# A local-attention block with a gated feed-forward: the feed-forward's units in pairs, two first products and then two second ones, with the transposes between them

## The chip, the cores and the metric

The kernel runs on one core of one Trainium2 chip. The metric is the device time of one execution in microseconds (us); the figures given are medians of several runs. A profiled execution is one run of its own: its span counts from the first to the last instruction of the program, its time also has what lies around them.

## The reference

`x` has 2048 tokens of 640 features. It is normalised, and the result `xn` goes two ways: through a local attention (32 heads of 20 features, a window of 8 keys at every second position) with the output projection `wo`, and through a feed-forward with 1536 hidden features. The two are multiplied and added to `x`:

```python
xn = _layernorm(x)
s  = attention(xn @ wqkv) @ wo        # keys at pos - 2*w, w = 0..7
g  = silu( silu(xn @ w1) @ w2 )       # w1: 640 x 1536, w2: 1536 x 640
return x + s * g
```

All tensors are float32.

## The kernel before, in words

**Precision.** Each float32 operand is split into a high part rounded to the matmul type float32r and a low part (the rest). A product is three matmuls: high by high, low by high, high by low. Tiles come in such pairs: `TH`/`TL` (transposed normalised tokens, or transposed attention output), `SH`/`SL` (hidden features after silu), and a weight slot of the ring `WR` (seven slots, each with both halves of one weight unit).

**Groups.** The 2048 tokens are worked in four groups of 512 (four tiles of 128 rows). For each group TensorE does a qkv phase, from the second group on the `wo` phase of the group before, and then the feed-forward phase `ffn_phase`. After the last group comes the last `wo` product, `wo_last`. VectorE does the attention itself (long multiplies and reductions, L477 to L517) while TensorE is in the later phases.

**The feed-forward phase.** The hidden features go in 12 units of 128. For unit f there is a *first product* (below U): 15 matmuls of 512 columns into one PSUM bank of `ROT` (L786 to L788), with a slice of w1 as the stationary operand and `TH`/`TL` as the moving one. ScalarE then takes silu of the bank twice, into `SH[f % 2]` (rounded) and `SF[f % 2]` (exact), and VectorE subtracts the two into `SL[f % 2]` (L792 to L794). And there is a *second product* (below D): for each of the four token tiles, the stationary operand is 128 tokens of `SH` or `SL`, the moving one the 640 columns of w2's unit, in a matmul of 384 columns (L667) and one of 256 (L669), both in `tm_mm`. D has 16 matmuls with `SH` (`big`: by w2's high, then by its low half) and 8 with `SL` (`small`). All twelve D of a group accumulate in the same six PSUM banks of `ACC`, which ScalarE empties through silu into `G` at the end (L823).

**The order before.** U runs one unit ahead of D: U0, U1, D0, U2, D1, and so on to U11, D10, D11. In D the eight `small` matmuls come last, but for D11, where each token tile has its big and small ones together.

**Transposes.** Five chunks per group are transposed by four TensorE transposes each into a bank of `ROT` (L429 in `split_t`; below T), and leave it by a ScalarE copy into `TH` (L433) and a VectorE subtraction into `TL` (L434). In the first three groups they are the next group's normalised tokens, ahead of U7 to U11 (`XT_AT`). In the last group they are chunks of the attention output `O`, ahead of U8 to U11 and, for the fifth, ahead of D11 (`OL_AT`). `ROT` has two banks, taken in turn by U and T.

**Who sets the order.** Every operation is put on record with the tiles that it reads and writes. `Weave` plans starting times with a table of costs and then emits the instructions; TensorE keeps the order in which its work was recorded, the others are ordered by the plan and by priorities. Weight units are loaded in the order of the list `units`, seven ahead (`w_load`, called by `w_done` when a unit has been used); the first group loads raw weights, splits them on ScalarE and VectorE or GpSimd and stores them, later groups load the stored halves by GpSimd's queue (L363).

Of the kernel before, what the change touches and what calls it, by code (L numbers as in the profile page):

```python
# [8 lines left out]
F32 = mybir.dt.float32  # L9
F32R = mybir.dt.float32r  # L10
AF = mybir.ActivationFunctionType
OP = mybir.AluOpType
# [38 lines left out]
def tsl(t):  # L51
    return slice(t * P, (t + 1) * P)
# [120 lines left out]
def local_attention_silu_ffn(ctx: ExitStack, tc: tile.TileContext, x, wqkv, wo, w1, w2, out):  # L173
# [62 lines left out]
    def rot():  # L236
        i = take("rot", 2)
        return ROT[i], ("rot", i)
# [7 lines left out]
    def dve(n, fn, reads, writes, prio, lock=False):  # L246
        add("DVE", dv(n), fn, reads, writes, prio, lock)

    def act(n, fn, reads, writes, prio, table=None):
        add("ACT", ac(n), fn, reads, writes, prio, table=table)  # L250

    def pe(dur, fn, reads, writes):
        add("PE", dur, fn, reads, writes)
        clock[0] += dur
# [22 lines left out]
    for g in range(NG):  # L277
        units += [("q", q, c) for q in range(NQ) for c in range(DC)]
        if g:
            units += [("wo", c) for c in range(DC)]  # L280
        for f in range(FC + 1):
            if f < FC:
                units.append(("w1", f))
            if f:
                units.append(("w2", f - 1))
    units += [("wo", c) for c in range(DC)]
    again = {u: sum(v == u for v in units) for u in units}
    halves = {}
# [97 lines left out]
    def w_next(*want):  # L386

        i = used[0]
        assert units[i] == want and i < loaded[0], (units[i], want)
        used[0] += 1  # L390
        s, n, at = i % RING, width(want), start(want)
        return WR[s][:, at:at + n], WR[s][:, D + at:D + at + n], ("wh", s), ("wl", s)

    def w_done(n=1):
        for _ in range(n):
            w_load()


    def load_x(g, t, n=1, prio=None):
        dma(lambda: nc.sync.dma_start(XIN[:, t:t + n], rows(xg, g)[:, t:t + n]), [],  # L400
            [("xin", u) for u in range(t, t + n)], n * P * D * 4, clock[0] if prio is None else prio)

    def ln_stats(t, after=()):
        st = ST[t % 2]
        ks = ("st", t % 2)
        for k in range(2):
            dve(320, lambda k=k: nc.vector.bn_stats(out=st[:, k, :], in_=XIN[:, t, k * 320:(k + 1) * 320]),
                [("xin", t), *after], [ks + (k,)], 1)
        dve(60, lambda: nc.vector.bn_aggr(out=MV[:, t, :], in_=st), [ks + (0,), ks + (1,)], [("mv", t)], 1)

    def ln_rstd(a, b, at=1):
        n = range(a, b)
        act(b - a, lambda: nc.scalar.activation(SD[:, 0, a:b], MV[:, a:b, 1], AF.Sqrt, bias=epst, scale=1.0),
            [("mv", t) for t in n], [("sd", t) for t in n], 0, "sqrt")
        dve(10, lambda: nc.vector.reciprocal(out=SD[:, 1, a:b], in_=SD[:, 0, a:b]),
            [("sd", t) for t in n], [("rs", t) for t in n], at)

    def ln_apply(t):
        dve(320, lambda: nc.vector.tensor_scalar(
            out=XIN[:, t, :], in0=XIN[:, t, :], scalar1=MV[:, t, 0:1], scalar2=SD[:, 1, t:t + 1],  # L420
            op0=OP.subtract, op1=OP.mult), [("rs", t), ("mv", t)], [("xin", t)], 1, lock=True)

    def split_t(src, skeys, c, i):

        ps, kp = rot()

        def turn():
            for t in range(T):
                nc.tensor.transpose(ps[:, tsl(t)], src[:, t, c * P:(c + 1) * P], ident)  # L429
        pe(0.54, turn, skeys, [kp])  # L430
        hi, lo = TH[i][:, c, :], TL[i][:, c, :]
        kh, kl = t_keys(i, [c], kinds=["th"]), t_keys(i, [c], kinds=["tl"])
        act(TOK, lambda: nc.scalar.activation(hi, ps, AF.Copy), [kp], kh, 0)  # L433
        dve(TOK, lambda: nc.vector.tensor_tensor(out=lo, in0=ps, in1=hi.bitcast(F32), op=OP.subtract),  # L434
            [kp] + kh, kl, 0)
# [85 lines left out]
    def o_chunk(g, c, i):  # L521
        qs = range(c * P // CQ, ((c + 1) * P - 1) // CQ + 1)
        split_t(O, [("o", q, t) for q in qs for t in (0, 2)], c, i)
# [127 lines left out]
    def t_keys(i, cs, ts=range(T), kinds=("th", "tl")):  # L651
        return [(k, i, c, t) for k in kinds for c in cs for t in ts]

    O_AT = {(1, 1): 0, (1, 4): 1, (2, 3): 2, (3, 1): 3, (3, 3): 4}
    OL_AT = {8: 0, 9: 1, 10: 2, 11: 3, 12: 4}
    XT_AT = 7

    def tm_banks():
        a = [bank() for t in range(T)]
        b = [bank() for t in range(T // 2)]  # L660
        return a, b
# [10 lines left out]
    def tm_views(banks):  # L672

        a, b = banks
        for k in range(T // 2):
            for t in (2 * k, 2 * k + 1):
                yield a[t][0][:, :CA].rearrange("p (t m) -> p t m", t=1), a[t][1], slice(t, t + 1), slice(0, CA)
            yield b[k][0].rearrange("p (t m) -> p t m", t=2), b[k][1], slice(2 * k, 2 * k + 2), slice(CA, D)
# [80 lines left out]
        leave(t, B)  # L759

    def ffn_phase(g, i, ix, io):
        nxt = g + 1 if g + 1 < NG else None
        ps = prev = None
        for f in range(FC + 1):
            if nxt is not None and f == 0:
                load_x(nxt, 0, 2)
                load_x(nxt, 2, 2)
                for t in range(T):
                    ln_stats(t)
                ln_rstd(0, T)  # L770
                for t in range(T):
                    ln_apply(t)
            if nxt is not None and XT_AT <= f < XT_AT + DC:
                split_t(XIN, [("xin", t) for t in range(T)], f - XT_AT, ix)
            if nxt is None and f in OL_AT:
                o_chunk(g, OL_AT[f], io)
            cur = None
            if f < FC:
                wh, wl, kh, kl = w_next("w1", f)
                h, kp = rot()  # L780
                s = f % 2

                def first(wh=wh, wl=wl, h=h):
                    for c in range(DC):
                        cs = tsl(c)
                        nc.tensor.matmul(h, wh[:, cs], TH[i][:, c, :], start=c == 0, stop=False)  # L786
                        nc.tensor.matmul(h, wh[:, cs], TL[i][:, c, :], start=False, stop=False)  # L787
                        nc.tensor.matmul(h, wl[:, cs], TH[i][:, c, :], start=False, stop=c == DC - 1)  # L788
                pe(15 * mm(TOK), first, t_keys(i, range(DC)) + [kh, kl], [kp])
                w_done()  # L790
                sf, sh, sl = SF[s], SH[s], SL[s]
                act(TOK, lambda sh=sh, h=h: nc.scalar.activation(sh, h, AF.Silu), [kp], [("sh", s)], 0, "silu")  # L792
                act(TOK, lambda sf=sf, h=h: nc.scalar.activation(sf, h, AF.Silu), [kp], [("sf", s)], 0, "silu")
                dve(TOK, lambda sf=sf, sh=sh, sl=sl: nc.vector.tensor_tensor(  # L794
                    out=sl, in0=sf, in1=sh.bitcast(F32), op=OP.subtract), [("sf", s), ("sh", s)], [("sl", s)], 0, lock=True)
                cur = sh, sl, ("sh", s), ("sl", s)
            if f:
                sh, sl, ksh, ksl = prev
                if ps is None:
                    ps = tm_banks()  # L800
                a, b = ps
                wh, wl, kh, kl = w_next("w2", f - 1)
                for t in range(T):
                    def big(t=t, f=f, wh=wh, wl=wl, sh=sh):
                        tm_mm(ps, t, sh[:, tsl(t)], wh, f == 1, False)
                        tm_mm(ps, t, sh[:, tsl(t)], wl, False, False)

                    def small(t=t, f=f, wh=wh, sl=sl):
                        tm_mm(ps, t, sl[:, tsl(t)], wh, False, f == FC)
                    ko = [a[t][1], b[t // 2][1]]  # L810
                    pe(2 * TM, big, [ksh, kh, kl], ko)
                    if f == FC:
                        pe(TM, small, [ksl, kh], ko)
                    else:
                        late.append((TM, small, [ksl, kh], ko))
                for args in late:
                    pe(*args)
                late.clear()
                w_done()
            prev = cur  # L820
        for p, kp, ts, cs in tm_views(ps):
            n = (ts.stop - ts.start) * (cs.stop - cs.start)
            act(n, lambda p=p, ts=ts, cs=cs: nc.scalar.activation(G[:, ts, cs], p, AF.Silu), [kp], gkeys(ts, cs), 0, "silu")  # L823

    late = []
    add("POOL", 0.7, consts, [], ["consts"], 0)
    act(1, lambda: nc.scalar.activation(SD[:, 1, 0:1], epst, AF.Sqrt), ["consts"], [("rs", 0)], 0, "sqrt")
    slot = 0
# [38 lines left out]
```

## Time and profile before

| | |
|---|---|
| median of 3 runs | 642.76 us (641.28 to 643.1) |
| profiled execution, time | 641.45 us |
| its span | 639.6 us |
| granted TensorE clock, mean over the span | 0.999 |
| busy: TensorE, weight loads, VectorE, ScalarE, GpSimd | 632.7, 572.5, 538.7, 207.2, 123.4 us |
| matmuls, transposes among them | 3495 |

The profiled execution has 1.85 us around its span. Records of matmuls overlap, since they are pipelined: the distance from one start to the next is the pace, the length of a record is not. In a line of the timeline the first number is the start, the second the length of the record, both in us; a line can stand for several instructions of a kind (x4).

### The profile page before, as it was taken

The numbers are of one execution on the slowest core, as the hardware profiler recorded it, in microseconds if no ns is written. First come the engines' busy times: TensorE is split into PE (matmuls) and PEld (weight loads), VectorE is DVE, ScalarE is ACT, GpSimd is POOL, SyncE is SP. The second block draws the span as 40 slices with busy tenths as digits, with TensorE's granted clock in tenths as the row PEclk, the third lists the DMA queues.
The fourth block names the chain that finished last, engine by engine and source line by source line (L and its number), as shares of the span: only waits on it lengthen the run. The fifth ranks groups of instructions, "written<-read, shape, count | busy, mean of one in ns | idle before, by whom it ended". The sixth has DMA issues, their size and how long they took to land.

```text
span 639.6 us, 9015 instructions
## 1 busy us (share of the span) xinstructions
PE 632.7 (99%) x3495; PEld 572.5 (90%) x3495; DVE 538.7 (84%) x539; ACT 207.2 (32%) x401; POOL 123.4 (19%) x168
## 2 busy tenths in 40 slices
PE   7999999999999999999999999999999999999997
PEld 6888889999889989999888999999988899899997
DVE  6699999999999989999839998999106999899814
ACT  4436453443534022324332112223313222233230
POOL 4500000001101241111222125111222213411100
PEclk9999999999999999999999999999999999999999
DMA  9999999777999998657699978865679995885522
GB/s 280 338 306 318 335 403 378 293 233 225 282 328 323 291 303 256 194 167 214 183 267 276 291 219 272 304 186 165 170 208 258 285 301 194 270 305 185 186 83 82
DMA packets 74154, 162.44 MB, mean 254 GB/s; under 512 B 5648, under 2 KB 47088, under 8 KB 74112
## 3 DMA queue, kind: packets, MB, share of 16 engines
q0 software_dynamic: 26672, 82.58, 44.9%
q1 hardware_dynamic: 47040, 79.05, 39.7%
q8 instruction: 27, 0.44, 0.3%
q10 hardware_dynamic: 400, 0.25, 0.1%
q14 instruction: 15, 0.12, 0.1%
HBM read 109.55 MB, written 34.16 MB: 225 GB/s over the span
## 4 chain that ended last, share of the span: by engine, by line
PE 98%; DVE 1%; DMA 1%; ACT 0%; issue 0%; SPq 0%
PE acc L667 22%; PE acc L669 15%; PE acc L633 10%; PE acc L634 10%; PE acc L635 10%; PE rot L788 9%; PE rot L786 9%; PE rot L787 9%; PE rot L429 2%; PE acc L579 2%; DMA xin<-in_A_x_dram 1%; PE rot L756 0%; DVE xin L549 0%; PE rot L558 0%; DVE st L544 0%; ACT th L562 0%
## 5 line engine op out<-in xcount | busy, mean ns | idle before, releaser
L633 PE MATMUL acc<-w,th 128*128 128x480 f32 x300 | 114.7, 382 | 0.0
L667 PE MATMUL acc<-w,sh 128*128 128x384 f32 x384 | 113.6, 335 | 0.0
L634 PE MATMUL acc<-w,tl 128*128 128x480 f32 x300 | 113.5, 378 | 0.0
L635 PE MATMUL acc<-w,th 128*128 128x480 f32 x300 | 113.4, 378 | 0.0
L669 PE MATMUL acc<-w,sh 128*128 128x256 f32 x384 | 107.1, 279 | 0.0
L477 DVE TENSOR_TENSOR pr<-q,kv 128x2560 f32<-128x2560 f32 x32 | 90.3, 2821 | 11.6 <-DMA kv<-kv 11.2
L786 PE MATMUL rot<-th,w 128*128 128x512 f32 x240 | 95.4, 398 | 0.0
L788 PE MATMUL rot<-th,w 128*128 128x512 f32 x240 | 94.0, 391 | 0.0
L787 PE MATMUL rot<-tl,w 128*128 128x512 f32 x240 | 93.9, 391 | 0.0
L509 DVE TENSOR_TENSOR pr<-e,kv 128x2560 f32<-128x2560 f32 x32 | 90.3, 2821 | 0.8
L480 DVE TENSOR_REDUCE l<-pr 128x128 f32<-128x2560 f32 x32 | 90.0, 2814 | 0.2
L363 POOL DMA_DIRECT2D w<-half_q x52 | 37.4, 719 | 233.3 <-DVE pr L514 93.5
L514 DVE TENSOR_TENSOR pr<-pr 128x1280 f32<-128x1280 f32 x64 | 76.6, 1197 | 1.1
L792 ACT ACTIVATE sh<-rot 128x512 fp32r<-128x512 f32 x48 | 28.8, 600 | 149.3 <-PE rot L788 146.6
L669 PEld LDWEIGHTS acc<-w,sh 128*128 128x128 f32 x384 | 72.3, 188 | 1.6
L667 PEld LDWEIGHTS acc<-w,sh 128*128 128x128 f32 x384 | 72.1, 188 | 1.7
L363 POOL DMA_DIRECT2D w<-half_w x72 | 38.6, 537 | 179.3 <-PE acc L669 96.4
L635 PEld LDWEIGHTS acc<-w,th 128*128 128x128 f32 x300 | 56.3, 188 | 8.5
L634 PEld LDWEIGHTS acc<-w,tl 128*128 128x128 f32 x300 | 56.4, 188 | 8.0
L633 PEld LDWEIGHTS acc<-w,th 128*128 128x128 f32 x300 | 56.3, 188 | 8.0
L667 PE MATMUL acc<-w,sl 128*128 128x384 f32 x192 | 57.8, 333 | 0.0
L434 DVE TENSOR_TENSOR tl<-rot,th 128x512 fp32r<-128x512 f32 x35 | 23.8, 681 | 38.3 <-ACT th L433 38.2
(88 smaller groups left out, 1002.9 us busy)
## 6 DMA issues: line engine op xcount, KB each, us to landing
w<-half_w POOLq DMA_DIRECT2D x72, 640.0 KB, 5.5
w<-half_q POOLq DMA_DIRECT2D x52, 480.0 KB, 5.1
half_w<-w SPq DMA_DIRECT2D x24, 640.0 KB
half_q<-w SPq DMA_DIRECT2D x20, 480.0 KB
w<-half_wo POOLq DMA_DIRECT2D x15, 640.0 KB, 5.4
kv<-kv SPq DMA_DIRECT2D x16, 560.0 KB
kv<-kv SPq DMA_DIRECT2D x16, 420.0 KB
gate<-in_B_w_dram SPq DMA_DIRECT2D x16, 320.0 KB
```

Source lines behind the costliest of these rows:

```text
L477: dve(2560, lambda t=t: nc.vector.tensor_tensor(out=PR, in0=win(qq[:, t:t + 2, :], W, 0), in1=win(kv[:, 0, t:t + 2, :], W, CQ), op=OP.mult ...
L480: dve(2560, lambda t=t: nc.vector.tensor_reduce(out=l[:, t:t + 2].rearrange("p t w h -> p (t w h)"), in_=PR.rearrange("p t w (h d) -> p (t ...
L509: dve(2560, lambda t=t, v=v: nc.vector.tensor_tensor(out=PR.rearrange("p t w (h d) -> p t (w h) d", d=DH), in0=e[:, t:t + 2].rearrange("p ...
L514: dve(2 * n * CQ, lambda n=n: nc.vector.tensor_tensor(out=PR[:, :, 0:n, :], in0=PR[:, :, 0:n, :], in1=PR[:, :, n:2 * n, :], op=OP.add), [] ...
L633: nc.tensor.matmul(o, hi, wh, start=c == 0, stop=False)
L634: nc.tensor.matmul(o, lo, wh, start=False, stop=False)
L635: nc.tensor.matmul(o, hi, wl, start=False, stop=c == DC - 1)
L667: nc.tensor.matmul(a[t][0][:, :CA], st, w[:, :CA], start=first, stop=last)
L669: nc.tensor.matmul(b[t // 2][0][:, h * CB:(h + 1) * CB], st, w[:, CA:], start=first and h == 0, stop=last, skip_group_check=True)
L786: nc.tensor.matmul(h, wh[:, cs], TH[i][:, c, :], start=c == 0, stop=False)
L787: nc.tensor.matmul(h, wh[:, cs], TL[i][:, c, :], start=False, stop=False)
L788: nc.tensor.matmul(h, wl[:, cs], TH[i][:, c, :], start=False, stop=c == DC - 1)
```

## The change

`ffn_phase` is written anew. The twelve units go in six pairs: U(f), U(f+1), D(f), D(f+1) for even f. A transpose that belongs to f stands between U(f+1) and D(f), one that belongs to f+1 between D(f) and D(f+1); `XT_AT` is now 6 to 10 and `OL_AT` 7 to 11, so that T stands ahead of D6 to D10 in the first three groups and ahead of D7 to D11 in the last. In the last pair of the first three groups the `small` matmuls of D10 are put off until after the `big` ones of D11. In the last group D11 has big and small matmuls of neighbouring token tiles in turn. The list `units`, and with it the order of the weight loads, follows the pairs. The matmuls, transposes and the work of the other engines are the same in number and shape.

```diff
-        for f in range(FC + 1):
-            if f < FC:
-                units.append(("w1", f))
-            if f:
-                units.append(("w2", f - 1))
+        for f in range(0, FC, 2):
+            units += [("w1", f), ("w1", f + 1), ("w2", f), ("w2", f + 1)]
...
-    OL_AT = {8: 0, 9: 1, 10: 2, 11: 3, 12: 4}
-    XT_AT = 7
+    OL_AT = 7, 8, 9, 10, 11
+    XT_AT = 6, 7, 8, 9, 10
...
+        def turns(at):
+            if nxt is not None and at in XT_AT:
+                split_t(XIN, [("xin", t) for t in range(T)], XT_AT.index(at), ix)
+            if nxt is None and at in OL_AT:
+                o_chunk(g, OL_AT.index(at), io)
...
+            if nxt is None and f == FC - 1:
+                order = [(big, 0)] + [v for t in range(1, T) for v in ((big, t), (small, t - 1))]
+            else:
+                order = [(big, t) for t in range(T)]
...
+        for f in range(0, FC, 2):
+            up(f)
+            up(f + 1)
+            turns(f)
+            rest = down(f)
+            if f < FC - 2 or nxt is None:
+                rest()
+            turns(f + 1)
+            last = down(f + 1)
+            if f == FC - 2 and nxt is not None:
+                rest()
+            last()
```

`up(f)` records U and the two silus and the subtraction; `down(f)` records D's big matmuls and returns `rest`, which records its small ones and marks the weight unit as used.

More of the change, by code (lines that the diff above doesn't have):

```diff
@@ L762, in ffn_phase @@
         nxt = g + 1 if g + 1 < NG else None
[L763 to L767, printed above, removed]
-                for t in range(T):
[L769 to L789, printed above, removed]
-                w_done()
[L791 to L820, printed above, removed]
@@ L821, in ffn_phase @@
-        for p, kp, ts, cs in tm_views(ps):
+        if nxt is not None:
+            load_x(nxt, 0, 2)
+            load_x(nxt, 2, 2)
+            for t in range(T):
+                ln_stats(t)
+            ln_rstd(0, T)
+            for t in range(T):
+                ln_apply(t)
+        def turns(at):
[3 more added lines that the diff above has]
+                o_chunk(g, OL_AT.index(at), io)
@@ new lines, in up, with first @@
+        def up(f):
+            wh, wl, kh, kl = w_next("w1", f)
+            h, kp = rot()
+            s = f % 2
+            def first():
+                for c in range(DC):
+                    cs = tsl(c)
+                    nc.tensor.matmul(h, wh[:, cs], TH[i][:, c, :], start=c == 0, stop=False)
+                    nc.tensor.matmul(h, wh[:, cs], TL[i][:, c, :], start=False, stop=False)
+                    nc.tensor.matmul(h, wl[:, cs], TH[i][:, c, :], start=False, stop=c == DC - 1)
+            pe(15 * mm(TOK), first, t_keys(i, range(DC)) + [kh, kl], [kp])
+            w_done()
+            sf, sh, sl = SF[s], SH[s], SL[s]
+            act(TOK, lambda: nc.scalar.activation(sh, h, AF.Silu), [kp], [("sh", s)], 0, "silu")
+            act(TOK, lambda: nc.scalar.activation(sf, h, AF.Silu), [kp], [("sf", s)], 0, "silu")
+            dve(TOK, lambda: nc.vector.tensor_tensor(out=sl, in0=sf, in1=sh.bitcast(F32), op=OP.subtract),
+                [("sf", s), ("sh", s)], [("sl", s)], 0, lock=True)
@@ new lines, in ffn_phase, with down, big, small @@
+        ps = []
+        def down(f):
+            if not ps:
+                ps.append(tm_banks())
+            a, b = ps[0]
+            s = f % 2
+            wh, wl, kh, kl = w_next("w2", f)
+            def big(t):
+                tm_mm(ps[0], t, SH[s][:, tsl(t)], wh, f == 0, False)
+                tm_mm(ps[0], t, SH[s][:, tsl(t)], wl, False, False)
+            def small(t):
+                tm_mm(ps[0], t, SL[s][:, tsl(t)], wh, False, f == FC - 1)
+            out = [[a[t][1], b[t // 2][1]] for t in range(T)]
+            def give(what, t):
+                if what == big:
+                    pe(2 * TM, lambda: big(t), [("sh", s), kh, kl], out[t])
+                else:
+                    pe(TM, lambda: small(t), [("sl", s), kh], out[t])
+            if nxt is None and f == FC - 1:
+                order = [(big, 0)] + [v for t in range(1, T) for v in ((big, t), (small, t - 1))]
+            else:
+                order = [(big, t) for t in range(T)]
+            for v in order:
+                give(*v)
+            def rest():
+                for t in range(T):
+                    if (small, t) not in order:
+                        give(small, t)
+                w_done()
+            return rest
@@ L822, in ffn_phase @@
+        for f in range(0, FC, 2):
[10 more added lines that the diff above has]
+            last()
+        done = ps[0]
+        for p, kp, ts, cs in tm_views(done):
             n = (ts.stop - ts.start) * (cs.stop - cs.start)
             act(n, lambda p=p, ts=ts, cs=cs: nc.scalar.activation(G[:, ts, cs], p, AF.Silu), [kp], gkeys(ts, cs), 0, "silu")
-    late = []
```

## The prediction

> **What bounds the kernel now.** I read the page's busy shares first, then the chain that ended last, then the waits of TensorE (PE).
>
> ```profile
> span 639.6 us, 9015 instructions
> PE 632.7 (99%) x3495; PEld 572.5 (90%) x3495; DVE 538.7 (84%) x539; ACT 207.2 (32%) x401; POOL 123.4 (19%) x168
> PE 98%; DVE 1%; DMA 1%; ACT 0%; issue 0%; SPq 0%
> ```
>
> ```profile
> PE rot L558 <- DVE xin L549: 1.5, 2, 0.8
> PE rot L532 <- POOL ident masks.py:199: 1.4, 1, 1.4
> PE acc L579 <- DVE tl L566: 0.3, 1, 0.3
> ```
>
> The chain is PE for 98% of the span, and every wait of PE (3.2 us in all) is at L532, L558 and L579, in the start of the first group. In the four feed-forward phases PE waits for nobody. So there is no stall for the new order to remove. Its time can only move by the pace of the matmuls (distance from start to start) or by new waits. The granted clock is 0.999, so the clock isn't the lever either.
>
> Does the pace depend on the order? I went through the timeline of PE, in the trace's starts to the ns (the view prints 10 ns). It does, and the pattern repeats from unit to unit within 2 ns:
>
> - U after a D: 3446 ns (15 matmuls; the first nine start 224 to 236 ns apart, the rest 226 to 227).
> - U after a U: only U1 after U0 shows it. The two together take 6824 ns, and the 15 matmuls of U1 keep 226.6 throughout: 3399.
> - D after a U: 2307 for the big part and 1147 for the small, 3454. The first three pairs of a 384 and a 256 take about 293 each, the others 286.6.
> - D after a D: D11 in the first three groups, twelve pairs at 286.6: 3440.
> - T ahead of U: 355 for the transposes and then 3518 for U, 3873 in all.
> - T ahead of D: once in the whole trace, ahead of D11 of the last group, and it looks different:
>
> ```profile
> 613.87 0.33 PE L667 MATMUL acc<-w,sl 128*128 128x384 f32 x1
> 614.04 0.28 PE L669 MATMUL acc<-w,sl 128*128 128x256 f32 x1
> 614.15 0.60 PE L429 MATMUL rot<-ident,o 128*128 128x128 f32 x4
> 614.51 0.42 PE L667 MATMUL acc<-w,sh 128*128 128x384 f32 x1
> 614.77 0.28 PE L669 MATMUL acc<-w,sh 128*128 128x256 f32 x1
> 614.89 0.34 PE L667 MATMUL acc<-w,sh 128*128 128x384 f32 x1
> ...
> 617.59 0.34 PE L667 MATMUL acc<-w,sh 128*128 128x384 f32 x1
> 617.77 0.28 PE L669 MATMUL acc<-w,sh 128*128 128x256 f32 x1
> 617.89 0.34 PE L667 MATMUL acc<-w,sl 128*128 128x384 f32 x1
> 618.07 0.28 PE L669 MATMUL acc<-w,sl 128*128 128x256 f32 x1
> 618.19 0.34 PE L667 MATMUL acc<-w,th 128*128 128x384 f32 x1
> ```
>
> From T's first start (614.15) to the first matmul of the last `wo` product (618.19) pass 4.04 us, to the ns 4036. After the transposes the first pair takes 382 ns, and from 614.89 to 618.19 eleven pairs take 300 each, against 286.6 for such pairs elsewhere. The pace does not recover within the unit. The order inside this D11 isn't the cause: the D11 of the other groups have the same one, come right after D10, and run at 286.6. I read it as a lasting pace: a D that starts right after transposes stays 13.4 ns per pair slow, some 160 ns per unit.
>
> **The sum, part by part.** The model reproduces the phase before. Groups 0 to 2: 6824 + 5 x 3446 (U2 to U6) + 5 x 3873 (T and U7 to U11) + 11 x 3454 (D0 to D10) + 3440 = 84.85 us, and the next group's first matmul does start 84.85 after this phase's (219.80 to 304.65). Last group: 6824 + 6 x 3446 + 4 x 3873 + 11 x 3454 + 4036 = 85.02, as seen (533.17 to 618.19).
>
> *Pairs.* Groups 0 to 2 have U0 and U1 as before, 6824, and five pairs at 3446 + 3399 = 6845. The three D pairs without a T take 3454 + 3440 = 6894 each. That saves 47 ns for each of five U that now follow a U, and 14 for each D that now follows a D.
>
> *Transposes.* T goes from ahead of U to ahead of D6 to D10, at 4036 each, by the one row there is. D11 then follows D10 without transposes between; I let it keep the slow pace, 12 x 300 = 3600. The trace has T ahead of D after a D (here D7 and D9) and not after a U (D6, D8, D10). Bounds for the latter: 4036, and 3890 (355 + 382 + 11 x 286.6) if that pace is left at once. I take 4036, since T's own starts (108 or 109 apart, the last 28 or 29) are the same after a U-sized matmul, a qkv one or a D.
>
> Groups 0 to 2: 6824 + 5 x 6845 + 3 x 6894 + 5 x 4036 + 3600 = 85.51, so +0.66 each. Last group: 6824 + 5 x 6845 + 4 x 3454 (D0, D2, D4, D6) + 3 x 3440 + 5 x 4036 (D7 to D11) = 85.36, +0.34. In all 3 x 0.66 + 0.34 = +2.3 us: the pairs alone save, the five places of T cost more. The U after a slow D could enter cheaper (U0 and U1 after the `wo` phase take 6824, 21 less than 6845): 8 x 0.02 = 0.17 us, left in the range.
>
> *Waits that the order could add*, all taken at nothing, with their cover. Counted from the end of U's last record, before the change `SH` is ready after 0.64 to 2.41 us over all 48 units and `SL` after 1.85 to 5.29. D's big part used to start 6.7 us after it; now it starts after 3.24 (U 3.40 less the 0.16 by which the record outlasts the next start), and the small part 2.31 later, after 5.54. Margins: 0.8 us for `SH`, 0.25 for the worst `SL`. In the last pair of groups 0 to 2 D10's small part is put off, so D11 needs `SH` after 0.36 + 8 pairs (2.49) - 0.16 = 2.69, against 2.41 at worst. `ROT`: T ahead of D6 takes the bank of U6, whose silus end 1.1 to 2.9 us after U6, during U7. U8 takes it two D later. At the end of a group D10's and D11's small parts finish together 1.2 us before qkv, where D11's tiles used to finish one by one. ScalarE empties a 384 bank in 0.49 and a 512 one in 0.60. By these qkv's tiles, 0.65 us apart, find their four banks free since about 0.3, 0.5, 0.1 and 0.4 us. In the last group D11's turns leave `wo_last` its first two banks about when it asks; a wait here is 0.2 at most. Weights: a slot is used seven units after its load was asked for, some 20 us, and a load lands 5.5 us after its issue. The new `units` order and the later `w_done` of D10 (2.3 us) shift GpSimd's loads and SP's raw loads by at most one unit, 3.5 us. If a cover is gone, the price is the wait itself, since PE runs in order and all else of the phase is queued behind it.
>
> A rule speaks against any effect of the pairs. The Trainium skill, in "TensorE: Matmul & The Clock Gate", section "Wait — 56ns, not 53.3ns?", gives the start-to-start time of warm matmuls as their columns at 2.4 GHz plus a fixed 2.5 ns or so, whatever stands around them. By it the order is free and the sum is 0. The trace disagrees: the same 512-column matmul takes up to 236 or 226.6 ns by what came before.
>
> **Against which time.** The profiled execution took 641.45 us, 639.6 of it span; by its own time the changed kernel takes 643.8. It lies 1.3 under the median of 642.76, at the low end of the three runs, so I put the change on the median: 642.76 + 2.3 = 645.1 us. A measurement of this kernel tells about 0.3%, 1.9 us, from no change.
>
> **The rivals.**
>
> *The slow pace does not come, or not after a U* (0.22). For it: D0 to D10 leave their first slow pairs after three; one row is thin. Without it D6 to D10 cost 3890 and D11 3440. I keep the last group's D11 at 4036, as measured. Then groups 0 to 2 change by -0.235 us each and the last by 0.34 - 4 x 0.146 = -0.24: -0.95 in all, 641.8. If it comes only ahead of D7, D9 and the last D11: +0.2, 643.0. Both are within 0.3%.
>
> *The pace knows no order* (0.05): each matmul keeps one distance whatever comes before, nothing moves, 642.8. The rows above (236 and 226.6 for one shape) speak against it. This is what the rule of the Trainium skill's "TensorE: Matmul & The Clock Gate" would make of the change.
>
> *VectorE becomes late* (0.12). Its queue is in order, and it is 84% busy, much of it with multiplies that cannot be interrupted. The page's group of one of them (32 of 2.82 us), and all 48 subtractions into `SL` (shortest, median and longest in ns):
>
> ```profile
> L477 DVE TENSOR_TENSOR pr<-q,kv 128x2560 f32<-128x2560 f32 x32 | 90.3, 2821 | 11.6 <-DMA kv<-kv 11.2
> ```
>
> ```profile
> L794 DVE TENSOR_TENSOR sl<-sf,sh x48: 676/686/1969, 68.7 to 612.1; 128x512 fp32r<-128x512 f32 x48
> ```
>
> With 0.25 us left at worst, one more 2.82 us multiply ahead of a subtraction costs up to 2.6 us. It decides once `SL` is later than 5.54 us. At half of 2.6 once per group it adds 5.2, some 650. Against it: only 3 of the 48 units are later than 4.8 us before.
>
> *Faster* (0.08): T is cheaper ahead of D than the one row says. If the first pair after T came at its usual pace (287 for 382) and no slow pace followed, 19 new places of T ahead of D would save 0.095 each more than in the first rival: -0.95 - 1.8 = -2.75, 640.0. It decides from an extra under about 45 ns. For it: a D's first weights are ready long before. Against it: 382 at 614.51, and U after T has a first distance of 316 too.
>
> **How the numbers follow.** The forecast has the rest, 0.53. Its 2.3 us are just over the bound (2.1 with the cheaper U), so I count 0.46 of it as slower and 0.07 as the same. Slower: 0.46 + 0.12 = 0.58. Same: 0.07 + 0.22 + 0.05 = 0.34. Faster: 0.08. The range runs from 641.4 (the first rival, less 0.4 for the spread of the runs) to 648.0 (the forecast with one wait of 2.6 us, and the spread); it leaves out the faster case and most of the late VectorE. The likeliest case alone is 644.2 to 646.0.
>
> **What would show it.** In the changed trace: U's second of a pair at 3.40 us; twelve pairs at 300 ns in D6 to D11, 85.5 us from a phase's first matmul to the next phase's, and no wait of PE outside the first group. I am wrong if D after T runs at 286.6, if PE waits for `sl`, `sh` or `gate`, or if a phase is shorter than 84.85.

## The result and the profile after

| | before | after |
|---|---|---|
| median of 5 runs, us | 642.75 (641.28 to 643.1) | 646.28 (645.68 to 647.09) |
| ratio, 95% interval | | 1.0063 (1.0053 to 1.0074) |
| profiled execution, us | 641.45 | 645.68 |
| its span, us | 639.6 | 643.9 |

The change makes the kernel slower by 3.5 us in the medians. The forecast was 645.1, 2.3 us slower, in a range of 641.4 to 648.0. The two profiled executions lie 4.2 us apart. Each is at the low end of its kernel's runs, so what follows adds up to the 4.3 us between the spans and not to the 3.5 between the medians.

The page of the changed kernel, its first lines and the head of the chain (up to the feed-forward its line numbers are 3 lower: L664 and L666 are D's matmuls, L426 is T; U is L784 to L786, the subtraction into `SL` L792):

```profile
span 643.9 us, 9007 instructions
PE 635.3 (99%) x3495; PEld 574.6 (89%) x3495; DVE 536.3 (83%) x539; ACT 204.9 (32%) x401; POOL 128.6 (20%) x168
PE 79%; DVE 14%; issue 2%; DMA 2%; ACT 1%; SPq 1%; DVEq 0%
```

PE was 98% of the chain before. Now VectorE (DVE) has 14% of it: somewhere PE waits for it. The waits of PE (line, for whom, us in all, times, the longest) say where; the first, third and fifth were there before:

```profile
PE rot L555 <- DVE xin L546: 1.4, 2, 0.8
PE acc L664 <- DVE sl L792: 1.4, 2, 0.8
PE rot L529 <- POOL ident masks.py:199: 1.4, 1, 1.4
PE acc L630 <- ACT q L440: 0.3, 1, 0.3
PE acc L576 <- DVE tl L563: 0.3, 1, 0.3
```

New are two waits for `SL` in the feed-forward and one of a qkv phase for a PSUM bank. As listed they are 1.7 us of the 4.3. The four feed-forward phases of the changed kernel, from the first matmul of U0 to the first of the next phase (start:end, its length, then busy us of PE, weight loads, VectorE, ScalarE and GpSimd, the granted clock, DMA share and GB/s):

```profile
63.07:148.40 85.33, 85.33 (x489) 77.96 (x488) 81.72 (x77) 37.96 (x63) 3.02 (x4) 1.00 0.89 318
220.23:305.53 85.30, 85.30 (x490) 77.97 (x489) 79.11 (x77) 25.35 (x40) 23.24 (x28) 1.00 0.69 217
377.40:463.78 86.38, 85.75 (x491) 78.20 (x490) 71.79 (x64) 23.73 (x39) 23.01 (x28) 1.00 0.66 207
536.17:622.44 86.27, 85.47 (x490) 77.93 (x489) 71.97 (x64) 24.63 (x40) 20.91 (x27) 1.00 0.64 208
```

They were 84.88, 84.85, 84.85 and 85.02. The first two lose 0.46 and 0.45 us without any wait. That is the pace, as the forecast had it. The timeline inside D7 of the first group, which started right after transposes:

```profile
117.95 0.34 PE L664 MATMUL acc<-w,sl 128*128 128x384 f32 x1
118.13 0.28 PE L666 MATMUL acc<-w,sl 128*128 128x256 f32 x1
118.25 0.34 PE L664 MATMUL acc<-w,sl 128*128 128x384 f32 x1
118.43 0.28 PE L666 MATMUL acc<-w,sl 128*128 128x256 f32 x1
118.55 0.34 PE L664 MATMUL acc<-w,sl 128*128 128x384 f32 x1
```

From one 384-column matmul to the next it takes 0.30 us, for 0.287 in D0 to D5 of this group. Every D of the three first groups from D6 on ends at this pace, D11 (not preceded by transposes) too.

The third and fourth phase lose 1.52 and 1.25 us. In both, D4 waits between its big and its small part (first the third group, then the matmul that waited in the fourth):

```profile
413.88 0.28 PE L666 MATMUL acc<-w,sh 128*128 128x256 f32 x1
414.79 0.45 PE L664 MATMUL acc<-w,sl 128*128 128x384 f32 x1 [0.63 <-DVE sl L792]
415.07 0.28 PE L666 MATMUL acc<-w,sl 128*128 128x256 f32 x1
415.19 0.34 PE L664 MATMUL acc<-w,sl 128*128 128x384 f32 x1
...
573.73 0.45 PE L664 MATMUL acc<-w,sl 128*128 128x384 f32 x1 [0.80 <-DVE sl L792]
```

In the third group the next start comes 910 ns later instead of 116 (the bracket counts only from the end of the last record). VectorE's queue at that time shows why:

```profile
408.46 2.81 DVE L477 TENSOR_REDUCE l<-pr 128x128 f32<-128x2560 f32 x1
411.30 2.83 DVE L474 TENSOR_TENSOR pr<-q,kv 128x2560 f32<-128x2560 f32 x1
414.05 1.29 DVE L792 TENSOR_TENSOR sl<-sf,sh 128x512 fp32r<-128x512 f32 x2
```

The page's group of these multiplies, and all 48 subtractions into `SL`, as shown for the kernel before:

```profile
L474 DVE TENSOR_TENSOR pr<-q,kv 128x2560 f32<-128x2560 f32 x32 | 90.3, 2821 | 14.1 <-DMA kv<-kv 13.7
```

```profile
L792 DVE TENSOR_TENSOR sl<-sf,sh x48: 628/689/2059, 68.6 to 615.7; 128x512 fp32r<-128x512 f32 x48
```

Their lengths are what they were; only the place in the queue differs. U4 ended at 408.45. ScalarE had to load its silu table first (1.28 us) and gave `SF` at 410.9. By then the reduction of 2.81 was running and the multiply of 2.83 stood next in the queue, so the subtraction for U4 ended at 414.73, 6.3 us after U4; the wanted 5.5 had passed. In the fourth group it is 6.5. In the kernel before, U4 of the third group ended at 404.17, and its subtraction had one such multiply and three short instructions ahead of it. It was done 4.8 us after U4, in time for D4, which came later there:

```profile
404.10 2.82 DVE L477 TENSOR_TENSOR pr<-q,kv 128x2560 f32<-128x2560 f32 x1
...
408.24 0.69 DVE L794 TENSOR_TENSOR sl<-sf,sh 128x512 fp32r<-128x512 f32 x1
```

Last, the qkv phase of the last group is 0.57 us longer. ScalarE's queue there:

```profile
504.27 0.42 ACT L489 ACTIVATE e<-l 128x256 f32<-128x256 f32 x1 [11.39 <-DVE l L487]
504.59 0.58 ACT L430 ACTIVATE th<-rot 128x512 fp32r<-128x512 f32 x1
505.07 0.43 ACT L437 ACTIVATE kv<-acc 128x320 f32<-128x320 f32 x1
505.39 0.31 ACT L440 ACTIVATE q<-acc 128x160 f32<-128x160 f32 x1
```

The exp (L489) waits for VectorE's scores, and the copies that empty PE's banks stand behind it. The Trainium skill says in "TensorE: Matmul & The Clock Gate", section "Architectural detail: the array is 16× 32×32, not 1× 128×128", that ScalarE and VectorE take their queues strictly in order; both places agree with it. VectorE's first scores of that phase start 27.4 us after the phase's start, for 24.3 before.

The sum between the spans: pace about 1.5 (0.46 + 0.45 + 0.45 + 0.16), the two waits for `SL` with what follows them about 2.2 (1.07 + 1.09), the qkv phases 0.6.

### The profile page after: what moved, and what is told of

Same layout as the page of the kernel before. It is cut to its first block, busy times and chain, and to the rows that moved or that the text cites. A ratio compares the mean times of both kernels' runs of the same rounds, so it can differ in the third digit from the quotient of the medians.

```text
span 643.9 us, 9007 instructions
## 1 busy us (share of the span) xinstructions
PE 635.3 (99%) x3495; PEld 574.6 (89%) x3495; DVE 536.3 (83%) x539; ACT 204.9 (32%) x401; POOL 128.6 (20%) x168
## 4 chain that ended last, share of the span: by engine, by line
PE 79%; DVE 14%; issue 2%; DMA 2%; ACT 1%; SPq 1%; DVEq 0%
PE acc L664 18%; PE acc L666 12%; PE acc L630 8%; PE acc L632 8%; PE acc L631 8%; PE rot L785 7%; PE rot L786 7%; PE rot L784 7%; DVE l L477 3%; DVE pr L474 3%; DVE pr L506 2%; PE acc L576 2%; PE rot L426 2%; DVE pr L511 2%; DMA kv<-kv 2%
## 5 line engine op out<-in xcount | busy, mean ns | idle before, releaser
L664 PE MATMUL acc<-w,sh 128*128 128x384 f32 x384 | 116.0, 341 | 0.0
L666 PE MATMUL acc<-w,sh 128*128 128x256 f32 x384 | 107.7, 280 | 0.0
L786 PE MATMUL rot<-th,w 128*128 128x512 f32 x240 | 93.6, 390 | 0.0
L784 PE MATMUL rot<-th,w 128*128 128x512 f32 x240 | 93.5, 390 | 0.0
L511 DVE TENSOR_TENSOR pr<-pr 128x1280 f32<-128x1280 f32 x64 | 75.2, 1175 | 1.1
L666 PEld LDWEIGHTS acc<-w,sh 128*128 128x128 f32 x384 | 72.3, 188 | 0.5
L664 PEld LDWEIGHTS acc<-w,sh 128*128 128x128 f32 x384 | 72.1, 188 | 0.5
L664 PE MATMUL acc<-w,sl 128*128 128x384 f32 x192 | 58.7, 339 | 1.4 <-DVE sl L792 1.4
L792 DVE TENSOR_TENSOR sl<-sf,sh 128x512 fp32r<-128x512 f32 x48 | 35.6, 746 | 23.8 <-ACT sf L791 23.7
```

The source lines that it names most:

```text
L511: dve(2 * n * CQ, lambda n=n: nc.vector.tensor_tensor(out=PR[:, :, 0:n, :], in0=PR[:, :, 0:n, :], in1=PR[:, :, n:2 * n, :], op=OP.add), [] ...
L664: nc.tensor.matmul(a[t][0][:, :CA], st, w[:, :CA], start=first, stop=last)
L666: nc.tensor.matmul(b[t // 2][0][:, h * CB:(h + 1) * CB], st, w[:, CA:], start=first and h == 0, stop=last, skip_group_check=True)
```

## The experiments

**Is it the place of the transposes?** One run takes them out of the pairs of the first three groups, one puts them ahead of D in the order of before.

`e1`, on the changed kernel:

```diff
-    XT_AT = 6, 7, 8, 9, 10
+    XT_AT = 2, 4, 6, 8, 10
...
+            if nxt is not None:
+                turns(f)
             up(f)
             up(f + 1)
-            turns(f)
+            if nxt is None:
+                turns(f)
```

> The changed kernel with the transposes T of the first three groups ahead of the first U of the pairs from U2 on (U2, U4, U6, U8, U10) instead of ahead of D6 to D10; the last group stays as changed. Theory (a D that starts after transposes runs at 300 ns a pair, a U does not): in groups 0 to 2 every D is back at 3.45 us, U after T takes 3.87 with its T, a phase takes 84.55 us where the changed kernel has 85.3, so about 2.3 us less than the changed kernel in the sum over three groups, 644.0, as long as no new wait comes. Rival (the place of T does not matter, the pairs' waits carry the cost): 646.3 as the changed kernel. Known risk of the edit: the second U of a pair uses the bank of T and may wait for VectorE's subtraction out of it; such waits are to be read off the profile.

Measured: 644.99 us, ratio to the kernel before 1.0050 (1.0037 to 1.0063). The third group has no wait that the view lists, and there the expected pace is seen:

```profile
379.59:464.26 84.67, 84.67 (x491) 77.21 (x490) 70.69 (x64) 23.91 (x38) 21.00 (x28) 1.00 0.66 211
```

84.67 where the kernel before has 84.85: without a T ahead of a D the pairs do save. The expected 84.55 is missed because in two pairs the second U takes 0.13 us longer, together, than in the others. The known risk came true, too, and more. In the first group the second U of a pair waits twice for the bank of T (about 1 us together). In the second, qkv waits 1.1 us for the banks that ScalarE empties at the end. In the last, which kept the changed order, D4 waits for `SL` as before. So the place of T decides the pace, and this order buys it with other waits.

`e2`, on the kernel before:

```diff
-            if nxt is not None and XT_AT <= f < XT_AT + DC:
-                split_t(XIN, [("xin", t) for t in range(T)], f - XT_AT, ix)
-            if nxt is None and f in OL_AT:
-                o_chunk(g, OL_AT[f], io)
             cur = None
             if f < FC:
...
                 cur = sh, sl, ("sh", s), ("sl", s)
+            if nxt is not None and XT_AT <= f < XT_AT + DC:
+                split_t(XIN, [("xin", t) for t in range(T)], f - XT_AT, ix)
+            if nxt is None and f in OL_AT:
+                o_chunk(g, OL_AT[f], io)
             if f:
                 sh, sl, ksh, ksl = prev
```

> The kernel before with its order of U and D kept and only T moved, from ahead of U(f) to between U(f) and D(f-1). Theory: each T with its D takes about 4.01 us (0.355 + 3.65) and the U after it 3.41, against 3.87 + 3.45 before: +0.09 us for each of 19 places, +1.7 us, 644.5, with no wait of the tensor engine in the feed-forward phases. Rival (T's place is free): 642.8. Rival (the cost comes with the shorter slack of the pairs alone): 642.8 as well, and D after T at 286.6 ns a pair.

Measured: 644.90 us, ratio 1.0046 (1.0033 to 1.0059). The phases take 85.53, 85.85 (with one new wait for `sl` of 0.4), 85.49 and 85.41. The first of them:

```profile
63.00:148.53 85.53, 85.53 (x489) 77.90 (x488) 81.69 (x77) 39.19 (x64) 3.03 (x4) 1.00 0.91 324
```

Each of the 19 moved T takes 353 ns, its D 2454 + 1200 and the U behind 3410 or so; the price of 0.09 us each is as expected. I had left out D11, which keeps the slow pace and adds 0.16 in the first and the third group; in the second it is back at 286.6 after the wait. No order of before has been touched but T's, and the loss of pace is all there: it belongs to D after transposes, not to the pairs.

**What makes D slow?** In `e4` each T transposes its last tile twice:

```diff
-            for t in range(T):
+            for t in (*range(T), T - 1):
                 nc.tensor.transpose(ps[:, tsl(t)], src[:, t, c * P:(c + 1) * P], ident)
```

> The changed kernel with the last transpose of every T in the feed-forward and qkv phases done twice (the same result), five where there were four. If the slow pace of D belongs to the point of time at which D starts against something periodic, 109 ns more in front of it lead to another pace (286.6 or 293 ns a pair) in at least some D. If it belongs to any D that follows transposes, all of D6 to D10 keep 300 and the kernel takes 0.11 us more for each of 35 T, some 3.8 us more than the changed kernel.

Measured: 648.90 us (one run), and the pace is now mixed. D6 of the first group in its timeline:

```profile
112.33 0.71 PE L426 MATMUL rot<-ident,xin 128*128 128x128 f32 x5
112.80 0.42 PE L664 MATMUL acc<-w,sh 128*128 128x384 f32 x1
113.06 0.28 PE L666 MATMUL acc<-w,sh 128*128 128x256 f32 x1
113.18 0.33 PE L664 MATMUL acc<-w,sh 128*128 128x384 f32 x1
113.35 0.28 PE L666 MATMUL acc<-w,sh 128*128 128x256 f32 x1
113.46 0.33 PE L664 MATMUL acc<-w,sh 128*128 128x384 f32 x1
```

From 113.18 to 113.46 a pair takes 0.286: no slow pace, right after five transposes. In the first two groups D6, D8 and D10 (T after a U) run so to their end, and D11 with them; D7 and D9 (T after a D) still go into 300. The first two phases take 85.35 and 85.36 us, the same as with four transposes, although 5 x 0.109 = 0.54 us of transposes were added to each. So transposes as such do not slow D. It has two paces that it can keep, and what decides is how it starts.

A few ns may be enough. In the third group D6 goes into 300 in spite of its five transposes. There T starts 237 ns after the start of U7's last matmul, where it is 230 in the first two groups. One other T in all the runs starts 237 ns behind a U, the one ahead of D6 in the first group of `e3` (below). That D6 goes into 300, but D7, right behind the next four transposes, runs at 286.6:

```profile
114.43 0.60 PE L426 MATMUL rot<-ident,xin 128*128 128x128 f32 x4
...
115.17 0.33 PE L664 MATMUL acc<-w,sh 128*128 128x384 f32 x1
115.34 0.28 PE L666 MATMUL acc<-w,sh 128*128 128x256 f32 x1
115.46 0.33 PE L664 MATMUL acc<-w,sh 128*128 128x384 f32 x1
```

That the 7 ns do it is argued from these two places; no run set them on purpose.

`e6` turned the pair around for D, on the changed kernel, in `tm_mm` (the three calls in D pass `turned=True`):

```diff
...
+        if turned:
+            nc.tensor.matmul(b[t // 2][0][:, h * CB:(h + 1) * CB], st, w[:, CA:], start=first and h == 0,
+                             stop=last, skip_group_check=True)
+            nc.tensor.matmul(a[t][0][:, :CA], st, w[:, :CA], start=first, stop=last)
+            return
         if 0 in cols:
             nc.tensor.matmul(a[t][0][:, :CA], st, w[:, :CA], start=first, stop=last)
...
```

> The changed kernel with the 256-column matmul ahead of the 384-column one in every pair of D. If the slow pace is a matter of where D's first matmul falls, D after T starts 53 ns differently into its pattern and may run at 286.6 ns a pair: then the phases of groups 0 and 1 take about 84.5 us for 85.3. If any D after T is slow whatever its order: 300 ns a pair, 85.3.

Measured: 647.91 us (one run). In the first two groups the roles change. D7 and D9 run at 286.6 (2388 ns in their big part), D6, D8 and D10 at 300, and now even D0 to D5, with no T near them, fall into 300 (2380 and 2400). The phases of groups 0 and 1 take 85.97 and 85.94. This fits the reading that the place of D's first matmul matters, but it does not show it alone, since the edit turns every pair of D around as well. The hoped-for 84.5 did not come. What the starting point has to fit is not settled: the records show the two paces, not their cause.

**Are the waits for `SL` part of the change?** `e3`, on the changed kernel:

```diff
-            if f < FC - 2 or nxt is None:
+            late = nxt is not None or f < FC - 2
+            if not late:
                 rest()
             turns(f + 1)
             last = down(f + 1)
-            if f == FC - 2 and nxt is not None:
+            if late:
                 rest()
```

> The changed kernel with the small matmuls of the first D of every pair put off until after the big ones of the second D, as the change does in the last pair only. It gives SL of the first unit 2.3 us more. Theory (two waits for SL at D4 in groups 2 and 3 cost 2.1 us with what follows them): the phases of groups 2 and 3 take 85.4 and 85.2 us where the changed kernel has 86.4 and 86.3, PE waits for no sl, 644.2. Rival (pace alone makes the loss, the waits were of that one execution): 646.3 as the changed kernel. SH of the second unit is wanted 2.3 us after its U, a wait for sh of 0.1 to 0.3 may come where ScalarE loads a table.

Measured: 644.22 us, ratio 1.0032 (1.0019 to 1.0044), 2.1 us less than the changed kernel, as expected. The two phases in question:

```profile
378.10:463.40 85.30, 85.30 (x490) 77.97 (x489) 71.50 (x64) 23.73 (x39) 23.15 (x28) 1.00 0.64 209
536.14:621.37 85.23, 85.23 (x490) 77.95 (x489) 71.77 (x64) 24.62 (x40) 21.36 (x27) 1.00 0.63 210
```

86.38 and 86.27 have become 85.30 and 85.23, with no wait in them. The waits are the shorter way from U to the small part of D. They weren't an accident of one execution either: `e4` and `e5`, which keep that way, have them at the same D4 in the same two groups (904 to 917 ns). The feared waits for `sh` did not come. Waits for banks outside the feed-forward did: 0.37 us at the start of the first `wo` phase and 0.91 in the last qkv phase.

**The wait in qkv.** `e5`, on the changed kernel:

```diff
-            if f < FC - 2 or nxt is None:
-                rest()
+            rest()
             turns(f + 1)
             last = down(f + 1)
-            if f == FC - 2 and nxt is not None:
-                rest()
             last()
```

> The changed kernel without putting off the small matmuls of D10 in the first three groups: every D does its big and its small part at once. Theory on the wait in the last qkv phase (ScalarE's copies out of the banks stand behind an exp that waits for VectorE, whose first scores start 27.4 us after the phase's start instead of 24.3): if the two weight loads that the put-off issues 1.2 us apart delay the halo copies, the scores are back at 24 to 25 us and the wait of 0.6 us is gone. Rival (the halo copies land late for another reason): 26.5 to 27.5 us and a wait as in the changed kernel. The pace and the two waits for SL at D4 stay either way: 645.7 or 646.3.

Measured: 646.33 us, ratio 1.0065 (1.0050 to 1.0080). The first scores are back at 25.0 us after the phase's start in both later groups, and the qkv phase is 71.83 us between the feed-forwards, as before. That fits: in the changed kernel the put-off small part frees two weight slots together, and their loads go out at 463.05 and 464.24 instead of 3.4 us apart. This is 13 us ahead of the copies that the scores wait for. Yet the loads behind the two are issued at the same points of the phase as in `e5` and land later, by 0.3 to 1.2 us, and the last one ahead of the copies, issued 0.2 us before the first of them, lands 22.7 us after the phase's start instead of 17.8. The other profiles side with it: in the last group the five with the put-off (the changed kernel, `e1`, `e3`, `e4`, `e6`) have their first scores 26.3 to 27.8 us after the phase's start, the four without (the kernel before, `e2`, `e5`, `e7`) 24.3 to 25.1. With the put-off that load lands at 22.4 to 23.3, without it at 17.8 to 18.8. In the third group the scores do not divide so: 25.4 to 27.7 with the put-off, 25.0 to 26.2 without. That the put-off makes them late is shown for the last group; that it does so through the two loads fits these landings and is argued. The median did not fall with it: 646.33 is the number of the rival. The two waits at D4 stay, and in the profiled execution the start of the first group took 1 us longer (64.07 for 63.07); whether it does in the other executions is not shown.

**A version from the price list.** Pairs where no T is due, T only ahead of a U, the small part of a pair's first D put off so that `SL` has time. `e7`, on the changed kernel (the list `units` follows the new order, and D11 has the order of the kernel before; both are left out below, and so are the lines of the old loop):

```diff
...
+        for f in (0, 2, 4):
+            up(f)
+            up(f + 1)
+            rest = down(f)
+            last = down(f + 1)
+            rest()
+            last()
+        turns(6)
+        up(6)
+        up(7)
+        down(6)()
+        for f in range(8, FC):
+            turns(f - 1)
+            up(f)
+            down(f - 1)()
+        turns(FC - 1)
+        down(FC - 1)()
```

> A version that the runs point to: pairs for U0 to U5 with the small part of each pair's first D put off, then the order of the kernel before, with every T ahead of a U (U6, U8 to U11; in the last group U8 to U11 and D11 as before). By the rows: groups 0 to 2 at 84.67 us, the last at 84.85, against 84.85 and 85.02: 0.7 us less than the kernel before, 642.0, too little for its measurement to tell. A wait of U7 for the bank of T in the first group, up to 1.3 us, would use that up. Rival (the shorter slack of the pairs makes waits whatever the place of T): 643 to 644.

Measured: 641.63 us over 11 runs, ratio to the kernel before 0.9992 (0.9983 to 1.0001). Its four phases:

```profile
63.67:148.36 84.69, 84.69 (x489) 77.38 (x488) 81.50 (x77) 39.19 (x64) 3.03 (x4) 1.00 0.94 329
220.28:304.93 84.65, 84.65 (x490) 77.38 (x489) 81.34 (x84) 26.86 (x42) 21.05 (x28) 1.00 0.73 225
376.77:461.42 84.65, 84.65 (x491) 77.38 (x489) 71.42 (x64) 25.16 (x40) 20.53 (x28) 1.00 0.68 217
533.25:618.07 84.82, 84.82 (x490) 77.53 (x489) 70.66 (x64) 25.19 (x40) 18.87 (x27) 1.00 0.65 211
```

84.67 three times and 84.85 had been summed up from the rows; the phases are 84.69, 84.65, 84.65 and 84.82, and PE waits only in the start of the first group. It is the fastest of all versions here, by 0.7 us, and even so its interval just touches no change.

## Why the prediction was right, and where it was not

**The direction and its mechanism** were right: nothing to gain but pace, pairs that save 47 and 14 ns, transposes ahead of D that cost more. U after U measured 3399, D after D 2293 + 1147, both as in the list. `e2` and `e7` show the two parts by themselves.

**The terms of the pace** were too high. T with its D takes 4007 after a U and 4012 after a D that is slow already, not 4036: it needs five or six pairs to fall into 300 where the single row of before went there at once. That row holds for its own case, T after a D at 286.6: the one such place of the changed kernel, D7 of the last group, takes 4037. U after a slow D takes 3410, not 3446; the cheaper entry that I had left in the range is real and larger, 0.04 instead of 0.02. Together +0.45 per group instead of +0.66, and +0.16 instead of +0.34 in the last: 1.5 us for 2.3. That the U before T changes nothing in kind (the open bound of 3890 or 4036) was right, though the row it leans on, T's starts after "a U-sized matmul", is not in the trace: there T stands behind matmuls of 480 and 256 columns only.

**The waits taken at nothing** are the step that failed. "Margins: 0.8 us for `SH`, 0.25 for the worst `SL`" took the lateness of `SL` in the old order as if it carried over. But the queue of VectorE is planned anew for the new order. After U4, where ScalarE reloads its table, a multiply of 2.83 us got ahead of the subtraction, and 5.29 us at worst became 6.3 and 6.5. This is the rival of the late VectorE, held at 0.12, with its mechanism as written; it came in two groups of four, 1.1 us each where I had counted 1.3 in every group. "PE waits for `sl`" was also one of the signs that I had named for being wrong. Also, the weights' step "shift ... by at most one unit" looked only at whether the weights come in time, and not at what the loads do to the halo copies and so to the scores, the exp and the banks behind it: 0.6 us (that the two loads together do it is argued, see `e5`).

**The total** is therefore right partly by luck. A pace term 0.8 us too high hid a part of 2.7 us of waits put at zero. Between the spans the change costs 4.3 us, 2.0 more than the forecast; between the medians 3.5, and 646.28 lies inside the range but above the 644.2 to 646.0 of the likeliest case alone.

**The rule that the order is free** is refuted here: one and the same pair of matmuls runs at 286.6 or at 300 ns in one kernel, at a granted clock of 1.00. The Trainium skill, in "TensorE: Matmul & The Clock Gate", section "Wait — 56ns, not 53.3ns?", gives a fixed cost per warm matmul on top of its columns, measured on back-to-back matmuls; "whatever stands around them" was my reading of it, and it does not hold for trains of mixed sizes.

## What to carry to other kernels

When the tensor engine is busy 98% of the chain, read the starts of its matmuls to the nanosecond and make a price list by what stands ahead of each unit: here it gave the phases of a new order to 0.03 us (`e7`). A slack read off the old order is no cover for a new one where a queue is planned anew: find the longest instruction that can get in front and subtract it. And transposes are best put where the product behind them recovers by itself, here the one with 512 columns.

## What the runs showed of the hardware

A train of matmuls of 384 and 256 columns can keep either of two paces, 286.6 or 300 ns a pair, for as long as it lasts (12 to 24 pairs here), with the same shapes, tiles and clock. Which one depends on how it starts. With the 384 first, four transposes ahead led to 300 in 86 of 87 D; five led to 286.6 behind a U (10 of 11) and to 300 behind a D (9 of 9, `e4`). With the 256 first, four led to 300 behind a U (11 of 11) and to 286.6 behind a D (9 of 9, `e6`). A stop of the engine can do it as well: after the wait at D4 the third group went on at 300 and the fourth, at the same place, at 286.6. What in the start decides stays open. The 512-column product fell back to 226.6 ns a matmul in every run, after a D within two to nine matmuls.
